# A Fourier, gated-MLP and sigmoid-MLP chain on one core: the mask copies one step earlier, the two readers of a first-layer bank swapped, and a Newton step in three operations

## The chip, the cores and the metric

One core of a Trainium2 chip runs one program. The metric is the device time of one execution in microseconds (us), median of the runs shown. TensorE (PE in the profile) multiplies matrices into PSUM banks, VectorE (DVE), ScalarE (ACT) and GpSimd (POOL) do the elementwise work, and SyncE (SP) issues most of the DMAs. Each engine works through its own list in order, and waits on semaphores for the others.

## The reference, cut to what matters

```python
X = fft(fft(x, axis=1), axis=2).real          # 4 x 3072 x 256
h = relu(X @ w_in)                            # 1024 columns
u, v = h[..., :512], h[..., 512:]
v_n = (v - mean(v)) / sqrt(var(v) + 1e-6)     # over the 512 columns
v_s = einsum('ts,bsd->btd', w_spatial, v_n) + b_spatial[None, :, None]
y = (u * v_s) @ w_out                         # 12288 tokens x 256
out = (sigmoid(y @ w_gate) * (y @ w_val)) @ w_out2
```

## The kernel before

Every fp32 product is made of three matmuls of a high and a low part (`mm3`, L260 to L262). The program has three stages: the Fourier transform with the first layer and its normalization, the spatial product (with `w_out`), and the second MLP. The change touches the first stage alone.

In the first stage the tokens of each of the four batches are handled in four units (3, 2, 0, 1, in this order). A unit has v blocks (128 tokens by 512 columns of v, PSUM tile `psv`) and u blocks (128 columns of u by 384 tokens, `psu`), alternating; one block is one step, 7 or 8 to a unit, 29 to a batch, 116 in all. The transform of real data is symmetric, so a unit holds pairs of tokens k and S - k: the sum of an even part E and an odd part O gives one token, and 2E - (E + O) gives the other. Each block therefore has three parts, that `put_off` spreads over the steps:

- at step n: `mm3` with the even part into the bank and one matmul for the few masked samples (`nt` by `g3`, L588 for a v block, L620 for a u block); ScalarE copies E out (`ev` L595, `eu` L622);
- at step n + 2 (`LAG`), `second`: `mm3` with the odd part adds into the same bank; then ScalarE reads the bank (L602 Relu for v, L628 copy for u), and VectorE reads it for the other token (`mirror`, L580);
- at step n + 3: for a v block `rest`, in which ScalarE puts the mirrored tile through Relu (L608) and VectorE takes the statistics of both tiles (`bn_stats`, L610); for a u block the store.

At the start of a unit ScalarE writes `nt`, a copy of the samples scaled by the batch's mask (L570, one buffer for all units). After a unit, `ln1`, `root` and `ln2` make the mean and the reciprocal root on tiles of 128x6 or 128x7: `y` starts as a reciprocal (L648), one Newton step refines it (L650 to L653), and `nm` is minus mean times `y` (L654). Then the tiles are normalized, the first and the last on ScalarE (L663), the others on VectorE (L659), and stored.

Between the blocks of one batch, the inputs of the next are folded on GpSimd (`fold_half`), split into parts (`split_one`: ScalarE casts `fh`, L255; for the third of a batch four copies `ex` come first, L345 to L348; GpSimd subtracts for `fl`, L256), and transformed (`fft`, `take_fft`). The numbers FOLDS, SPLITS, AT0 and the like give the steps at which these happen; nothing reorders them later. Two readers of one PSUM bank on different engines are put in order by semaphores: who comes first in the program reads first.

The spatial product starts on TensorE when the last block's second part is done (`bank` tiles); its first operands are prepared by `prepare_next` from step 103 on.

Of the kernel before, what the change touches and what calls it, by code (L numbers as in the profile page):

```python
# [10 lines left out]
F32R = mybir.dt.float32r  # L11
# [3 lines left out]
AF = mybir.ActivationFunctionType  # L15
ALU = mybir.AluOpType
# [8 lines left out]
P = 128  # L25
H = 384
R3 = H + 2
# [211 lines left out]
def tile_kernel(ctx: ExitStack, tc: tile.TileContext, t: dict, out: bass.AP):  # L239
    nc = tc.nc  # L240
# [9 lines left out]
    def f(ap):  # L250
        return ap.bitcast(F32)
# [66 lines left out]
    masks = keep.tile([P, 3 + B], F32, name="masks")  # L318
    gc = [keep.tile([P, 2, DFF], F32R, name=f"g{n}") for n in "hl"]
    g3 = keep.tile([P, DFF], F32R, name="g3")  # L320
    nts = [keep.tile([P, R3 if unit == 3 else H], F32R, name=f"nt{unit}") for unit in range(4)]
# [168 lines left out]
    for q, e in ((0, es), (1, xs[:, :, 1, :])):  # L490
        nc.scalar.copy(sps[:, :, q, :], e)
        nc.vector.scalar_tensor_tensor(
            out=sps[:, :, q, :], in0=f(sps[:, :, q, :]), scalar=masks[:, 2:3], in1=e, op0=ALU.mult, op1=ALU.add
# [63 lines left out]
    stp = pool(r0, "stp", 2, "right")  # L557
    vp = pool(r0, "vp", 13, "right")
    up = pool(r0, "up", 3, "right")

    def unit_blocks(pq, b, unit):

        (ph, pl), (qh, ql) = pq

        queue = nc.gpsimd if b == B - 1 and unit < 2 else nc.sync
        vsl = slice(DH, DFF)

        nt = stp.tile([P, R3], F32R, tag="nt", name="nt", bufs=1)
        nt = nt[:, : R3 if unit == 3 else H]
        nc.scalar.activation(nt, f(nts[unit]), AF.Identity, scale=masks[:, 3 + b : 4 + b])  # L570
        nb = 7 if unit == 3 else 6
        tiles = {}
        stats = stp.tile([P, 7, 6], F32, name="stats")
        mv = stp.tile([P, 7, 2], F32, name="mv")
        ve, sd, y, nm = (stp.tile([P, 7], F32, name=n) for n in ("ve", "sd", "y", "nm"))

        def mirror(to, part, ps):
            nc.vector.scalar_tensor_tensor(out=to, in0=part, scalar=2.0, in1=ps, op0=ALU.mult, op1=ALU.subtract)  # L580

        def v_block(m):

            w0 = m * P if m < 3 else R3 - P
            win = slice(w0, w0 + P)
            ps = ps_w.tile([P, 512], F32, tag="pa", name="psv")
            mm3(ps, (ph[:, win], pl[:, win]), (gc[0][:, 0, vsl], gc[1][:, 0, vsl]), True, False)
            nc.tensor.matmul(out=ps, lhsT=nt[:, win], rhs=g3[:, vsl], start=False, stop=True)  # L588
            if m == 3:
                tv = vp.tile([P, DH], F32, tag="tv", name="tv")  # L590
                nc.scalar.activation(tv, ps, AF.Relu)
                tiles[6] = tv
                return lambda: lambda: nc.vector.bn_stats(stats[:, 6, :], tv)
            ev = stp.tile([P, DH], F32, tag="e", name="ev", bufs=4)
            nc.scalar.copy(ev, ps)  # L595

            def second():
                weights = (gc[0][:, 1, vsl], gc[1][:, 1, vsl])
                mm3(ps, (qh[:, win], ql[:, win]), weights, False, True, skip_group_check=True)
                for sg in range(2):  # L600
                    tiles[sg * 3 + m] = vp.tile([P, DH], F32, tag="tv", name="tv")
                nc.scalar.activation(tiles[m], ps, AF.Relu)  # L602
                mirror(tiles[3 + m], ev, ps)
                return rest

            def rest():
                tv = tiles[3 + m]
                nc.scalar.activation(tv, tv, AF.Relu)  # L608
                for sg in range(2):
                    nc.vector.bn_stats(stats[:, sg * 3 + m, :], tiles[sg * 3 + m])  # L610

            return second

        def u_block(fb):

            fsl = slice(fb * P, fb * P + P)
            n = R3 if unit == 3 else H
            ps = ps_w.tile([P, 512], F32, tag="pa", name="psu")
            mm3(ps[:, :n], (gc[0][:, 0, fsl], gc[1][:, 0, fsl]), (ph[:, :n], pl[:, :n]), True, False)
            nc.tensor.matmul(out=ps[:, :n], lhsT=g3[:, fsl], rhs=nt[:, :n], start=False, stop=True)  # L620
            eu = stp.tile([P, R3], F32, tag="e", name="eu", bufs=4)
            nc.scalar.copy(eu[:, :n], ps[:, :n])  # L622

            def second():
                weights = (gc[0][:, 1, fsl], gc[1][:, 1, fsl])
                mm3(ps[:, :H], weights, (qh[:, :H], ql[:, :H]), False, True, skip_group_check=True)
                tu = up.tile([P, 2, H], F32, tag="tu", name="tu")
                nc.scalar.copy(tu[:, 0, :], ps[:, :H])  # L628
                mirror(tu[:, 1, :], eu[:, :H], ps[:, :H])
                if unit == 3:  # L630
                    nc.vector.tensor_copy(tu[:, 1, 0:1], eu[:, H : H + 1])
                at = u_d[b][:, fb, unit * 2 * H : unit * 2 * H + 2 * H]
                return lambda: queue.dma_start(at, tu.rearrange("p a k -> p (a k)"))

            return second

        a = slice(0, nb)

        def ln1():
            for i in range(nb):  # L640
                nc.vector.bn_aggr(mv[:, i, :], stats[:, i, :])
            nc.vector.tensor_scalar(out=ve[:, a], in0=mv[:, a, 1], scalar1=1e-6, scalar2=None, op0=ALU.add)

        def root():
            nc.scalar.activation(sd[:, a], ve[:, a], AF.Sqrt)

        def ln2():
            nc.vector.reciprocal(y[:, a], sd[:, a])  # L648

            nc.vector.tensor_tensor(out=sd[:, a], in0=y[:, a], in1=y[:, a], op=ALU.mult)  # L650
            nc.vector.tensor_tensor(out=sd[:, a], in0=sd[:, a], in1=ve[:, a], op=ALU.mult)
            nc.vector.tensor_scalar(out=sd[:, a], in0=sd[:, a], scalar1=-0.5, scalar2=1.5, op0=ALU.mult, op1=ALU.add)
            nc.vector.tensor_tensor(out=y[:, a], in0=y[:, a], in1=sd[:, a], op=ALU.mult)  # L653
            nc.vector.scalar_tensor_tensor(out=nm[:, a], in0=mv[:, a, 0], scalar=-1.0, in1=y[:, a], op0=ALU.mult, op1=ALU.mult)  # L654

        def norm(i):
            tv = tiles[i]
            if NORM_ON[i] != "a":
                engines[NORM_ON[i]].tensor_scalar(  # L659
                    out=tv, in0=tv, scalar1=y[:, i : i + 1], scalar2=nm[:, i : i + 1], op0=ALU.mult, op1=ALU.add  # L660
                )
            else:
                nc.scalar.activation(tv, tv, AF.Identity, scale=y[:, i : i + 1], bias=nm[:, i : i + 1])  # L663

        def store(i):
            tv = tiles[i]
            if i == 6:
                q = H - (R3 - P)
                queue.dma_start(v_d[b][0:1, unit * 6 + 3, :], tv[q : q + 1, :])
            elif unit == 3 and i == 3:  # L670

                for rows in (slice(16, P), slice(1, 16)):
                    queue.dma_start(v_d[b][rows, unit * 6 + i, :], tv[rows, :])
            else:
                queue.dma_start(v_d[b][:, unit * 6 + i, :], tv)

        def norms(i):
            for k in (i, i + 3):
                norm(k)
            for k in (i, i + 3):  # L680
                store(k)

        def last_norm():
            norm(6)
            store(6)

        blocks = []
        for i in range(4):
            if i < nb - 3:
                blocks.append(lambda i=i: v_block(i))  # L690
            blocks.append(lambda i=i: u_block(i))
        after = [root, ln2] + [lambda i=i: norms(i) for i in range(3)] + ([last_norm] if nb == 7 else [])
        return blocks, [ln1] + after
# [94 lines left out]
    units = [(b, unit) for b in range(B) for unit in (3, 2, 0, 1)]  # L788
# [41 lines left out]
    seconds, thirds, lns = {}, {}, {}  # L830
    step = 0

    def put_off(step, block=None):

        if block is not None:
            seconds[step + LAG] = block()
        if step in seconds:
            thirds[step + 1] = seconds.pop(step)()
        if step in thirds:
            thirds.pop(step)()  # L840
# [41 lines left out]
            for q in range(2):  # L882
                transform(base + AT3[q], b + 1, 3, q, pqs[b + 1, 3], None)
    transform(NYQ, B, 0, 0, None, None)
    for b, unit in units:
        blocks, later = unit_blocks(pqs[b, unit], b, unit)
        for block in blocks:
            put_off(step, block)
            for do in plan.pop(step, []):
                do()  # L890
            for first, _ in ffts.get(step, []):
                first()
            for do in lns.pop(step, []):
                do()
            for _, take in ffts.get(step, []):
                take()
            step += 1
        for k, do in enumerate(later):
            lns.setdefault(step + LAG + k, []).append(do)
# [457 lines left out]
```

## Time and profile before

| | us |
|---|---|
| median of 3 runs (2971.44 to 2974.28) | 2972.27 |
| the profiled execution | 2973.02 |
| its span | 2971.2 |
| PE busy | 2867.2 (96%) |
| DVE busy | 2064.7 (69%) |
| ACT busy | 1323.5 (45%) |
| POOL busy | 401.2 (14%) |

These are times of the whole span. The stages differ: TensorE is without pauses in the second and third, and VectorE is the busiest engine in the first. A share of the span thus says little on the change, and the rows below are taken from stretches of the first stage. "busy" is the time in which an engine executes, the idle time ahead of an instruction is put down to what ended it, and instructions of one engine overlap a little, so that the start of the next comes before the end of the last.

### The profile page before, as it was taken

The numbers are of one execution on the slowest core, as the hardware profiler recorded it, in microseconds if no ns is written. First come the engines' busy times: TensorE is split into PE (matmuls) and PEld (weight loads), VectorE is DVE, ScalarE is ACT, GpSimd is POOL, SyncE is SP. The second block draws the span as 40 slices with busy tenths as digits, with TensorE's granted clock in tenths as the row PEclk, the third lists the DMA queues.
The fourth block names the chain that finished last, engine by engine and source line by source line (L and its number), as shares of the span: only waits on it lengthen the run. The fifth ranks groups of instructions, "written<-read, shape, count | busy, mean of one in ns | idle before, by whom it ended". The sixth has DMA issues, their size and how long they took to land.

```text
span 2971.2 us, 34046 instructions
## 1 busy us (share of the span) xinstructions
PE 2867.2 (96%) x12550; PEld 2359.4 (79%) x12550; DVE 2064.7 (69%) x2908; ACT 1323.5 (45%) x2117; POOL 401.2 (14%) x408
## 2 busy tenths in 40 slices
PE   3888899999999999999999999999999999999999
PEld 2777788888878888888887888788888888888887
DVE  8898875768765765576666476866666666766665
ACT  3777532323232232332223233655555555555554
POOL 5774121122111002111002010000000000000000
PEclk8999999999999999999999999999999999999999
DMA  6565875778765776776876474200000000000000
GB/s 230 187 235 221 313 276 196 278 244 316 264 221 175 260 252 211 242 257 222 282 259 223 154 271 166 84 29 29 29 10 20 29 29 29 15 15 29 29 15 15
DMA packets 149656, 472.28 MB, mean 159 GB/s; under 512 B 16624, under 2 KB 18160, under 8 KB 149104
## 3 DMA queue, kind: packets, MB, share of 16 engines
q1 hardware_dynamic: 143712, 442.70, 43.2%
q0 software_dynamic: 2320, 14.82, 1.3%
q10 hardware_dynamic: 3456, 12.58, 1.1%
q8 instruction: 98, 1.61, 0.2%
q14 instruction: 70, 0.57, 0.1%
HBM read 387.46 MB, written 82.58 MB: 158 GB/s over the span
## 4 chain that ended last, share of the span: by engine, by line
PE 87%; DVE 8%; ACT 2%; issue 2%; DMA 1%; ACTq 0%; DVEq 0%; SPq 0%
PE bank L261 28%; PE bank L262 28%; PE bank L260 28%; DVE stats L610 1%; DVE gl L994 1%; DVE g L986 1%; ACT wh L751 1%; DVE st L747 1%; DVE tv L580 0%; DVE wl L754 0%; DVE tu L580 0%; DMA v_d<-tv 0%; PE psv L588 0%; DVE tv L659 0%; PE psf L260 0%
## 5 line engine op out<-in xcount | busy, mean ns | idle before, releaser
L262 PE MATMUL bank<-wh,vl 128*128 128x512 f32 x2016 | 786.3, 390 | 0.0
L261 PE MATMUL bank<-wl,vh 128*128 128x512 f32 x2016 | 786.0, 390 | 0.0
L260 PE MATMUL bank<-wh,vh 128*128 128x512 f32 x2016 | 785.4, 390 | 0.0
L754 DVE TENSOR_TENSOR wl<-st,wh 128x1024 fp32r<-128x1024 f32 x252 | 331.4, 1315 | 390.9 <-ACT wh L751 388.9
L751 ACT CAST wh<-st 128x1024 fp32r<-128x1024 f32 x252 | 265.2, 1053 | 594.6 <-PE bank L262 351.6
L260 PEld LDWEIGHTS bank<-wh,vh 128*128 128x128 f32 x2016 | 379.3, 188 | 79.9
L261 PEld LDWEIGHTS bank<-wl,vh 128*128 128x128 f32 x2016 | 379.1, 188 | 80.0
L262 PEld LDWEIGHTS bank<-wh,vl 128*128 128x128 f32 x2016 | 378.9, 188 | 79.0
L1240 DVE TENSOR_TENSOR t<-t,bank 128x512 f32<-128x512 f32 x144 | 99.0, 688 | 250.3 <-PE bank L262 250.2
L747 POOL TENSOR_TENSOR st<-st 128x1024 f32<-128x1024 f32 x60 | 156.5, 2608 | 812.9 <-DMA st<-v_d 512.2
L261 PE MATMUL bank<-x,wgh 128*128 128x512 f32 x673 | 265.9, 395 | 0.0
L262 PE MATMUL bank<-x,wgl 128*128 128x512 f32 x673 | 265.5, 395 | 0.0
L260 PE MATMUL bank<-x,wgh 128*128 128x512 f32 x673 | 264.1, 392 | 0.4 <-ACT t L1252 0.4
L747 DVE TENSOR_TENSOR st<-st 128x1024 f32<-128x1024 f32 x180 | 226.1, 1256 | 53.9 <-DMA st<-in_wt 53.9
L1261 DVE TENSOR_TENSOR gl<-s,gh 128x512 fp32r<-128x512 f32 x288 | 199.4, 693 | 57.4 <-ACT gh L1259 44.5
L262 PE MATMUL bank<-gh,wv 128*128 128x512 f32 x576 | 227.6, 395 | 0.0
L260 PE MATMUL bank<-gh,wv 128*128 128x512 f32 x576 | 226.8, 394 | 0.8 <-ACT gh L1254 0.8
L261 PE MATMUL bank<-gl,wv 128*128 128x512 f32 x576 | 225.8, 392 | 0.2 <-DVE gl L1261 0.2
L1231 ACT ACTIVATE s<-s 128x512 f32<-128x512 f32 x144 | 91.0, 632 | 149.0 <-DVE s L1230 149.0
L260 PEld LDWEIGHTS bank<-x,wgh 128*128 128x128 f32 x673 | 126.4, 188 | 31.2 <-ACT t L1252 0.8
L261 PEld LDWEIGHTS bank<-x,wgh 128*128 128x128 f32 x673 | 126.3, 188 | 30.6
L262 PEld LDWEIGHTS bank<-x,wgl 128*128 128x128 f32 x673 | 126.2, 188 | 28.6
(233 smaller groups left out, 4564.2 us busy)
## 6 DMA issues: line engine op xcount, KB each, us to landing
st<-in_wt SPq DMA_DIRECT2D x432, 512.0 KB, 5.3
st<-v_d SPq DMA_DIRECT2D x144, 512.0 KB, 4.9
u<-u_d SPq DMA_DIRECT2D x96, 256.0 KB, 4.4
u_d<-tu SPq DMA_DIRECT2D x56, 384.0 KB, 3.1
v_d<-tv SPq DMA_DIRECT2D x80, 256.0 KB, 2.5
xt<-in_xh SPq DMA_DIRECT2D x24, 512.0 KB, 4.6
x_d<-x ACTq DMA_DIRECT2D x24, 512.0 KB, 3.2
raw<-x_d SPq DMA_DIRECT2D x24, 512.0 KB, 4.5
```

The source lines that it names most:

```text
L260: nc.tensor.matmul(out=ps, lhsT=w[0], rhs=x[0], start=first, stop=False, **kw)
L261: nc.tensor.matmul(out=ps, lhsT=w[0], rhs=x[1], start=False, stop=False, **kw)
L262: nc.tensor.matmul(out=ps, lhsT=w[1], rhs=x[0], start=False, stop=last, **kw)
L610: nc.vector.bn_stats(stats[:, sg * 3 + m, :], tiles[sg * 3 + m])
L747: (nc.gpsimd if kind == "v" else nc.vector).tensor_tensor(out=tiles[0], in0=tiles[0], in1=tiles[1], op=ALU.add if sign > 0 else ALU.subtract)
L751: nc.scalar.copy(hl[0], tiles[0])
L754: lows.append(lambda: nc.vector.tensor_tensor(out=hl[1], in0=tiles[0], in1=f(hl[0]), op=ALU.subtract))
L986: nc.vector.scalar_tensor_tensor(out=g, in0=side["u"][d], scalar=0.0, in1=g, op0=ALU.max, op1=ALU.mult)
L994: side["low"] = lambda: nc.vector.tensor_tensor(out=gl, in0=g, in1=f(gh), op=ALU.subtract)
L1231: nc.scalar.activation(s1, s1, AF.Sigmoid)
L1240: nc.vector.tensor_tensor(out=g["t2"], in0=g["t2"], in1=g["b"], op=ALU.add)
L1261: nc.vector.tensor_tensor(out=l, in0=s, in1=f(h), op=ALU.subtract)
```

## The change

`own_samples` takes the writing of `nt` out of `unit_blocks`; it is called right behind the first part of the last block of the unit before (for the first unit ahead of the loop). In `second` of both kinds of block `mirror` stands ahead of ScalarE's read of the bank. The four operations of the Newton step become three, with the factor and the 1.5 folded into `scalar_tensor_tensor`.

```diff
@@ -558,16 +558,21 @@
     vp = pool(r0, "vp", 13, "right")
     up = pool(r0, "up", 3, "right")
 
+    nt_of = {}
+
+    def own_samples(b, unit):
+
+        nt = stp.tile([P, R3], F32R, tag="nt", name="nt", bufs=1)[:, : R3 if unit == 3 else H]
+        nc.scalar.activation(nt, f(nts[unit]), AF.Identity, scale=masks[:, 3 + b : 4 + b])
+        nt_of[b, unit] = nt
+
     def unit_blocks(pq, b, unit):
 
         (ph, pl), (qh, ql) = pq
 
         queue = nc.gpsimd if b == B - 1 and unit < 2 else nc.sync
         vsl = slice(DH, DFF)
-
-        nt = stp.tile([P, R3], F32R, tag="nt", name="nt", bufs=1)
-        nt = nt[:, : R3 if unit == 3 else H]
-        nc.scalar.activation(nt, f(nts[unit]), AF.Identity, scale=masks[:, 3 + b : 4 + b])
+        nt = nt_of.pop((b, unit))
         nb = 7 if unit == 3 else 6
         tiles = {}
         stats = stp.tile([P, 7, 6], F32, name="stats")
@@ -599,8 +604,8 @@
                 mm3(ps, (qh[:, win], ql[:, win]), weights, False, True, skip_group_check=True)
                 for sg in range(2):
                     tiles[sg * 3 + m] = vp.tile([P, DH], F32, tag="tv", name="tv")
+                mirror(tiles[3 + m], ev, ps)
                 nc.scalar.activation(tiles[m], ps, AF.Relu)
-                mirror(tiles[3 + m], ev, ps)
                 return rest
 
             def rest():
@@ -625,8 +630,8 @@
                 weights = (gc[0][:, 1, fsl], gc[1][:, 1, fsl])
                 mm3(ps[:, :H], weights, (qh[:, :H], ql[:, :H]), False, True, skip_group_check=True)
                 tu = up.tile([P, 2, H], F32, tag="tu", name="tu")
+                mirror(tu[:, 1, :], eu[:, :H], ps[:, :H])
                 nc.scalar.copy(tu[:, 0, :], ps[:, :H])
-                mirror(tu[:, 1, :], eu[:, :H], ps[:, :H])
                 if unit == 3:
                     nc.vector.tensor_copy(tu[:, 1, 0:1], eu[:, H : H + 1])
                 at = u_d[b][:, fb, unit * 2 * H : unit * 2 * H + 2 * H]
@@ -645,13 +650,13 @@
             nc.scalar.activation(sd[:, a], ve[:, a], AF.Sqrt)
 
         def ln2():
+            stt = nc.vector.scalar_tensor_tensor
             nc.vector.reciprocal(y[:, a], sd[:, a])
 
-            nc.vector.tensor_tensor(out=sd[:, a], in0=y[:, a], in1=y[:, a], op=ALU.mult)
-            nc.vector.tensor_tensor(out=sd[:, a], in0=sd[:, a], in1=ve[:, a], op=ALU.mult)
-            nc.vector.tensor_scalar(out=sd[:, a], in0=sd[:, a], scalar1=-0.5, scalar2=1.5, op0=ALU.mult, op1=ALU.add)
-            nc.vector.tensor_tensor(out=y[:, a], in0=y[:, a], in1=sd[:, a], op=ALU.mult)
-            nc.vector.scalar_tensor_tensor(out=nm[:, a], in0=mv[:, a, 0], scalar=-1.0, in1=y[:, a], op0=ALU.mult, op1=ALU.mult)
+            stt(out=ve[:, a], in0=y[:, a], scalar=-0.5, in1=ve[:, a], op0=ALU.mult, op1=ALU.mult)
+            nc.vector.tensor_tensor(out=ve[:, a], in0=ve[:, a], in1=y[:, a], op=ALU.mult)
+            stt(out=y[:, a], in0=ve[:, a], scalar=1.5, in1=y[:, a], op0=ALU.add, op1=ALU.mult)
+            stt(out=nm[:, a], in0=mv[:, a, 0], scalar=-1.0, in1=y[:, a], op0=ALU.mult, op1=ALU.mult)
 
         def norm(i):
             tv = tiles[i]
@@ -830,10 +835,12 @@
     seconds, thirds, lns = {}, {}, {}
     step = 0
 
-    def put_off(step, block=None):
+    def put_off(step, block=None, also=None):
 
         if block is not None:
             seconds[step + LAG] = block()
+            if also is not None:
+                own_samples(*also)
         if step in seconds:
             thirds[step + 1] = seconds.pop(step)()
         if step in thirds:
@@ -882,10 +889,11 @@
             for q in range(2):
                 transform(base + AT3[q], b + 1, 3, q, pqs[b + 1, 3], None)
     transform(NYQ, B, 0, 0, None, None)
-    for b, unit in units:
+    own_samples(*units[0])
+    for (b, unit), follows in zip(units, units[1:] + [None]):
         blocks, later = unit_blocks(pqs[b, unit], b, unit)
         for block in blocks:
-            put_off(step, block)
+            put_off(step, block, follows if block is blocks[-1] else None)
             for do in plan.pop(step, []):
                 do()
             for first, _ in ffts.get(step, []):
```

ScalarE at the end of batch 0's unit 0, the 7th and 8th row of each list being where `nt` for unit 1 (`nt1`) is written; `eu`, `tu` and `tv` are the copies of E, of u and of v. Before:

```order
L622 COPY eu_1058<-psu_1053 128x384 [waits DVE_49,PE_49]
L628 COPY tu_1063<-psu_1011 128x384 [waits DMAHW2_49,PE_49]
L608 ACTIVATE tv_1039<-tv_1039 128x512 [waits DMAHW7_49,DVE_49]
L663 ACTIVATE tv_759<-tv_759,nm_710,y_709 128x512 [waits DVE_49]
L622 COPY eu_1078<-psu_1073 128x384 [waits PE_49,Activation_49]
L602 ACTIVATE tv_1083<-psv_1028 128x512 [waits DMAHW0_49,PE_49]
L570 ACTIVATE nt_1092<-nt1_135,masks_130 128x384
L595 COPY ev_1105<-psv_1100 128x512 [waits DVE_49,PE_49]
L628 COPY tu_1110<-psu_1053 128x384 [waits DMAHW4_49,PE_49]
```

The same place of ScalarE's list now (numbers of buffers differ by a few):

```order
L627 COPY eu_1056<-psu_1051 128x384 [waits PE_49,Activation_49]
L634 COPY tu_1061<-psu_1010 128x384 [waits DMAHW2_49,DVE_49]
L613 ACTIVATE tv_1038<-tv_1038 128x512 [waits DMAHW6_49]
L668 ACTIVATE tv_759<-tv_759,nm_710,y_709 128x512 [waits DVE_49]
L627 COPY eu_1076<-psu_1071 128x384 [waits PE_49,Activation_49]
L566 ACTIVATE nt_1078<-nt1_135,masks_130 128x384
L608 ACTIVATE tv_1083<-psv_1027 128x512 [waits DMAHW1_49,DVE_49]
L600 COPY ev_1103<-psv_1098 128x512 [waits PE_49]
L634 COPY tu_1108<-psu_1051 128x384 [waits DMAHW4_49,DVE_49]
```

`nt` has moved up by one instruction, the Relu of a v tile; the normalization that waits for VectorE (L663, now L668) still stands ahead of it. The reads of `psu` and `psv` for `tu` and `tv` waited for PE and now wait for DVE.

VectorE at the same place; `stats` are the statistics of the two v tiles of one block, the second of which ScalarE has put through Relu (`tv_1039` before, `tv_1038` now) behind its copy of `tu`. Before:

```order
L580 SCALAR_TENSOR_TENSOR tu_1063<-eu_1016,psu_1011 128x384 [waits DMAHW2_49,Activation_49]
L610 BN_STATS stats_943<-tv_1038 128x6
L610 BN_STATS stats_943<-tv_1039 128x6 [waits Activation_49]
L659 TENSOR_SCALAR tv_760<-tv_760,y_709,nm_710 128x512 [waits DVE_49]
L580 SCALAR_TENSOR_TENSOR tv_1084<-ev_1033,psv_1028 128x512 [waits DMAHW1_49,Activation_49]
```

Now:

```order
L585 SCALAR_TENSOR_TENSOR tu_1061<-eu_1015,psu_1010 128x384 [waits DMAHW2_49,PE_49]
L615 BN_STATS stats_942<-tv_1037 128x6 [waits Activation_49]
L615 BN_STATS stats_942<-tv_1038 128x6 [waits Activation_49]
L664 TENSOR_SCALAR tv_760<-tv_760,y_709,nm_710 128x512 [waits DVE_49]
L585 SCALAR_TENSOR_TENSOR tv_1084<-ev_1032,psv_1027 128x512 [waits DMAHW0_49,PE_49]
```

VectorE's own order is the same. The mirrors waited for ScalarE and now wait for TensorE; the statistics, which follow at once, wait for ScalarE as before, and ScalarE's instructions ahead of that now wait for the mirror.

## Rows read from the trace of the kernel before

**Rows 1.** The page's span.

```profile
span 2971.2 us, 34046 instructions
```

**Rows 2.** Windows: stretch, its length, busy us by engine, PE clock, DMA share, GB/s.

```profile
200.00:300.00 100.00, 88.06 (x428) 78.94 (x427) 90.06 (x215) 72.18 (x146) 50.63 (x75) 0.95 0.61 221
...
1000.00:1500.00 500.00, 499.48 (x2198) 412.12 (x2197) 326.07 (x356) 146.77 (x168) 55.38 (x26) 1.00 0.72 243
```

**Rows 3.** Timeline of PE where the stages meet: start, duration, instruction [idle before <-releaser].

```profile
343.86 0.44 PE L260 MATMUL psu<-ph,gh 128*128 128x384 f32 x1 [1.71 <-ACT eu L622]
...
344.49 0.39 PE L260 MATMUL bank<-wh,vh 128*128 128x512 f32 x1
```

**Rows 4.** Timeline of ACT just before that.

```profile
342.63 0.81 ACT L663 ACTIVATE tv<-tv,nm,y 128x512 f32<-128x512 f32 x1 [0.79 <-DVE nm L654]
343.35 0.46 ACT L622 COPY eu<-psu 128x384 f32<-128x384 f32 x1
```

**Rows 5.** Timeline of DVE just before that.

```profile
342.43 0.17 DVE L654 SCALAR_TENSOR_TENSOR nm<-mv,y 128x6 f32<-128x6 f32 x1
```

**Rows 6.** Waits of DVE, 0 to 420 us: total us, times, longest us.

```profile
DVE tv L580 <- ACT tv L602: 19.0, 11, 3.4
DVE tu L580 <- ACT tu L628: 9.2, 13, 1.5
```

**Rows 7.** Waits of PE, 0 to 420 us.

```profile
PE psv L588 <- ACT nt L570: 34.3, 16, 6.3
```

**Rows 8.** Timeline of ACT at the end of batch 1's unit 0.

```profile
187.80 0.81 ACT L663 ACTIVATE tv<-tv,nm,y 128x512 f32<-128x512 f32 x1 [2.33 <-DVE nm L654]
...
188.88 0.60 ACT L602 ACTIVATE tv<-psv 128x512 f32<-128x512 f32 x1
189.37 0.61 ACT L570 ACTIVATE nt<-nt,masks 128x384 fp32r<-128x384 f32 x1
```

**Rows 9.** Timeline of PE at that place.

```profile
190.03 0.80 PE L588 MATMUL psv<-g,nt 128*128 128x512 f32 x1 [4.60 <-ACT nt L570]
```

**Rows 10.** Timeline of DVE, a mirror of u, two statistics, a mirror of v.

```profile
199.81 0.54 DVE L580 SCALAR_TENSOR_TENSOR tu<-eu,psu 128x384 f32<-128x384 f32 x1
200.28 1.27 DVE L610 BATCH_NORM_STATS2 stats<-tv 128x6 f32<-128x512 f32 x2
201.48 0.66 DVE L580 SCALAR_TENSOR_TENSOR tv<-ev,psv 128x512 f32<-128x512 f32 x1
```

**Rows 11.** Timeline of ACT, the copy of u and the Relu behind it.

```profile
207.48 0.48 ACT L628 COPY tu<-psu 128x384 f32<-128x384 f32 x1
207.86 0.64 ACT L608 ACTIVATE tv<-tv 128x512 f32<-128x512 f32 x1
```

**Rows 12.** Timeline of ACT, a cast that DVE waits for.

```profile
300.81 0.48 ACT L421 CAST ph<-psf 128x384 fp32r<-128x384 f32 x1 [1.65 <-DVE even L862]
```

**Rows 13.** Timeline of DVE, the instruction released by that cast.

```profile
301.32 0.56 DVE L422 TENSOR_TENSOR pl<-psf,ph 128x384 fp32r<-128x384 f32 x1 [0.55 <-ACT ph L421]
```

**Rows 14.** Lines, 60 to 345 us: count, ns min/median/max, first and last start.

```profile
L610 DVE BATCH_NORM_STATS2 stats<-tv x94: 668/679/691, 80.2 to 343.6; 128x6 f32<-128x512 f32 x94
L654 DVE SCALAR_TENSOR_TENSOR nm<-mv,y x15: 165/167/1147, 102.3 to 342.4; 128x6 f32<-128x6 f32 x11, 128x7 f32<-128x7 f32 x4
```

**Rows 15.** Timeline of DVE, two operations of a Newton step.

```profile
272.17 0.17 DVE L650 TENSOR_TENSOR sd<-y 128x6 f32<-128x6 f32 x1
272.37 0.17 DVE L651 TENSOR_TENSOR sd<-sd,ve 128x6 f32<-128x6 f32 x1
```

**Rows 16.** Timeline of DVE, the same operation beside GpSimd's work.

```profile
184.88 2.28 DVE L651 TENSOR_TENSOR sd<-sd,ve 128x6 f32<-128x6 f32 x1
```

**Rows 17.** Timeline of POOL at that place.

```profile
182.41 4.72 POOL L256 TENSOR_TENSOR fl<-fo,fh 128x1024 fp32r<-128x1024 f32 x2
```

**Rows 18.** Timeline of ACT, the cast behind the four copies of a split.

```profile
196.33 1.05 ACT L255 CAST fh<-fo 128x1024 fp32r<-128x1024 f32 x1
```

**Rows 19.** Timeline of DVE behind it.

```profile
198.39 0.69 DVE L580 SCALAR_TENSOR_TENSOR tv<-ev,psv 128x512 f32<-128x512 f32 x1 [2.94 <-ACT tv L602]
```

## The prediction

> **What bounds the kernel now.** I read the windows first. In the spatial product TensorE is busy for 499 of 500 us; in the first stage it is busy for 88 of 100 and VectorE for 90, with ScalarE at 72 [rows 2]. From the first `bank` matmul, at 344.49, TensorE has next to nothing to wait for [rows 2, 3]. So the change can only move that moment: what the first stage wins or loses is won or lost by the whole, and the 96% of TensorE's share tell nothing of it.
>
> Then I went back from that moment. The last second part waits for the copy of `eu` [rows 3], which ScalarE makes behind its normalization, which waits for `nm` of VectorE [rows 4, 5]. `nm` starts at 342.43 because VectorE comes to it then in its list. VectorE's progress therefore dates the end of the stage. Between 70 and 343 us it is nearly always at work, apart from 24 waits of 28.2 us in all ahead of a mirror, each for ScalarE's read of the same bank [rows 6].
>
> TensorE's waits for `nt` look larger, 34.3 us in 16 places [rows 7], but they are waits of an engine that runs ahead of the one that decides. They count only where VectorE then finds its bank unfinished.
>
> **Part 1: `nt` earlier.** The order shows `nt` moved up past one Relu of 0.60 and, where a transform is taken in the same step, past two casts as well. At the end of unit 0, where the largest stalls are, nothing else lies between: ScalarE stands at the normalization until 187.80, waiting 2.33 us for `nm`, and that is still ahead of `eu` and `nt` [rows 8]. So `nt` would start some 0.5 us earlier, at 188.88 for 189.37, and the 4.60 us stall [rows 9] keeps about 4.1. The added `nt` itself is no new work (16 before, 16 after); it now stands ahead of the Relu, which reaches the mirrored tile later by its 0.6. Value: 0.5 us at the about 8 of 16 boundaries where VectorE soon runs out of finished banks, 4 us gained. Bounds: 0, if VectorE is never short of banks, and 34.3.
>
> **Part 2: the mirror first.** What it removes: at each of the 24 waits the mirror no longer stands behind ScalarE's read. It still waits for TensorE, so where TensorE or ScalarE's backlog is late, only the read itself drops out: 0.48 for a copy [rows 11], 0.60 for a Relu [rows 8], with 0.03 for the hand-over (a cast starts at 300.81 and lasts 0.48, the next on VectorE starts at 301.32 [rows 12, 13]). 24 by 0.55 is 13.2 us. The upper bound is all 28.2.
>
> What it adds is not in the list of edits. Before, ScalarE ran ahead: it had copied u and put the mirrored v tile through Relu long before VectorE came to the mirror, and the two statistics ran behind it without a gap [rows 10]; no wait of the statistics is in the list of VectorE's waits. Now ScalarE's copy of u waits for the mirror of u, the Relu stands behind that copy, and the second statistic waits for the Relu. Put times to it from the mirror's start: mirror done at 0.54, copy started at 0.57, Relu 0.38 later at 0.95 [rows 11], done at 1.59, second statistic at 1.62. Without the wait it starts 0.47 (the mirror's) and 0.60 (half of 1.20 for the pair) after, at 1.07 [rows 10]. So each pair costs 0.55 us more on the engine that decides. There are 94 statistics in 47 pairs, 46 of them ahead of the last `nm` [rows 14]: 25.3 us. Behind VectorE's waiting statistic stand the next mirror and the normalizations; behind ScalarE's waiting copy stand the next `ev` or `eu`, which TensorE needs two steps later, so TensorE is not held. Some pairs lie where VectorE would have waited anyway; I take one in ten off: 23. Bounds: 0, if the idle places hide all, and 25.3.
>
> A rule bears on this. The hand-over from ScalarE to VectorE is seen at each of the 24 waits [rows 6]. The Trainium skill (PSUM — Partial Sum Buffer, section on bank collisions) says that two engines must not read one bank at the same time, that the hardware doesn't hold one back, and that software has to guard it. The trace agrees as far as it goes. Without such a guard both reads would start together, the new wait would be nothing, and the sum would be a gain of about 20; the order, in which ScalarE's read now waits for DVE, rules that out.
>
> Nor do all the long waits go. The wait of 2.94 at 198.39 [rows 19] stands behind ScalarE's four copies and its cast, which ends at 197.38 [rows 18]. The mirror can now start without them, at 195.45. But the next statistics need the Relu of the v tile, which stays behind that cast: 197.38, then some 0.5 for `ev` and 0.60 for the Relu, so the pair begins near 198.5, where before it began at 200.28 [rows 10]; its own 0.55 and a later start of the four copies (they now follow a copy of u that waits for a mirror) leave about 1 of the 2.94. This is why I take 13.2 and not 28.2.
>
> **Part 3: Newton.** Four operations become three. Their pace is 0.20 [rows 15], and a `scalar_tensor_tensor` of this shape has a median of 0.167 [rows 14], no more than the operations it replaces. 15 units come ahead of the last `nm`: 3.0 us gained. An operation of this step can also be held by GpSimd: 2.28 instead of 0.17, and it ended at 187.16, when GpSimd's two subtractions ended, at 187.13 [rows 15 to 17]. `nm`, a `scalar_tensor_tensor`, shows 1.147 at the most [rows 14], so the new form is not free of it. Bounds: 0, if VectorE merely reaches the next held operation sooner, and 3.0 and one such excess of 2.1.
>
> The Trainium skill (SBUF — State Buffer, Who interferes with whom) calls this an exclusive lock between GpSimd and a VectorE operation with two SBUF inputs. The three new operations still have two each; by that rule the excess stays and 3.0 is all, without it the excess of 2.1 would come on top.
>
> **The sum.** -4 (`nt`), -13.2 (old waits), -3.0 (Newton), +23 (new waits): 2.8 us slower. The profiled execution took 2973.02 (span 2971.2 [rows 1], the rest lies around it), 0.75 above the median of 2972.27. From it: 2975.8; on the median's scale 2975.
>
> **Rivals.**
>
> *The old waits really go.* If the 28.2 us vanish whole, with Newton's 3.0, and 15 of the new 25.3 remain, the change gains 16: 2956. For it: VectorE's waits are where it loses most, and its idle stretches can hide new waits. It also gives GpSimd free time in the new waits, and so fewer held operations. Against: the new waits, if they come at every pair, are nearly as long as all the old ones together, and they fall where VectorE is not idle now.
>
> *ScalarE in step with VectorE.* Slower: in the copies and casts of a split ScalarE cannot work ahead any more, since its copy of u waits for a mirror; the first statistic of the next pair waits about 2 us each of the three times, on top of all 46 new waits. 25.3 + 6 - 13.2 - 3.0 is 15 slower: 2987. It decides from the point where the pairs' waits pass the sum of what goes, 20 us, or 37 of 46 pairs at 0.55. For it: VectorE has 90 of 100 us of work. Against: the waits that go overlap with some of them.
>
> *`nt` doesn't come earlier.* TensorE's stalls at the end of unit 0 stay, because the normalization is still ahead, and `nt` gains nothing: -13.2 - 3.0 + 23, 6.8 slower: 2979. For it rows 8; against it that the other 12 boundaries have casts or more Relus ahead.
>
> **How the numbers follow.** The forecast has 50% (its own range 2966 to 2983), the first rival 20%, the second 20%, the third 10%. A measurement tells this kernel from no change by 0.2%, 5.9 us: 2966.3 to 2978.2 is the same. Of the forecast's half 40 points lie in there, 8 above, 2 below; the first rival gives 18 to faster and 2 to the same; the second all but 2 to slower; the third 4 to the same and 6 to slower. Faster 20%, same 48%, slower 32%. The range takes the forecast and the third whole and about half of the first and of the second: 2959 to 2987.
>
> **What would show it.** Waits of VectorE's statistics for ScalarE's Relu, near 46 of about 0.55, absent before. The waits ahead of mirrors nearly gone from the list. TensorE's waits for `nt` still there at the end of unit 0, above 3 us each, and below 1 us elsewhere. The first `bank` matmul near 347. Newton's operations three to a unit at a pace of 0.20. I am wrong if the statistics do not wait, if the stalls at the ends of unit 0 vanish with `nt`, or if the spatial product begins more than 6 us from 344.5; wrong in the premise if it begins where I say and the end moves otherwise.

## The result and the profile after

The changed kernel takes 2991.48 us (median of 4 runs, 2988.07 to 2993.9), the kernel before 2973.28 in the same comparison: a ratio of 1.0061, 95% interval 1.0043 to 1.0078, 18.2 us slower. The forecast was 2975, in a range up to 2987.

The loss is in the first stage. Its end, the first `bank` matmul, stood at 344.49 [rows 3]. After:

```profile
365.04 0.63 PE L260 MATMUL bank<-wh,vh 128*128 128x512 f32 x1
```

It comes 20.6 us later, and the span is 20.9 longer. VectorE's account of the stretch from 64 us to that moment, as windows (length, then busy us of PE, PEld, DVE, ACT, POOL), of the kernel before:

```profile
64.00:344.49 280.49, 236.22 (x1123) 210.89 (x1124) 236.53 (x547) 197.49 (x395) 150.05 (x227) 0.94 0.61 219
```

And after:

```profile
64.00:365.04 301.04, 245.33 (x1123) 215.52 (x1124) 233.01 (x536) 193.28 (x396) 150.34 (x229) 0.92 0.57 204
```

VectorE works 3.5 us less in all (236.53 to 233.01) and stands still 24.1 us more (43.96 to 68.03). TensorE has the same 1123 matmuls but is busy 9 us more, at a mean granted clock of 0.92 for 0.94: it waits 30 times, where it waited 23 times, and runs at the lower of its two levels behind some of them (1.2 GHz, a granted clock of 0.50, from 365.04 to 367, where the `bank` matmul takes 0.63 for 0.39). That alone is not the loss: newton_only, below, has 0.92 as well, and its first `bank` matmul comes at 344.39.

What VectorE waited for in that stretch after the change (total us, times, longest):

```profile
DVE stats L615 <- ACT tv L613: 25.1, 47, 1.5
DVE stats L615 <- ACT tv L608: 8.3, 6, 2.6
DVE pl L422 <- ACT ph L421: 8.0, 7, 3.4
DVE tv L585 <- PE psv L262: 6.3, 6, 2.9
...
DVE tu L585 <- PE psu L262: 2.4, 6, 0.7
DVE even L869 <- PE psf L262: 1.9, 2, 1.0
```

The 28.2 us of waits for ScalarE's reads of the banks [rows 6] are gone to the last one. The first line is the new wait of the pairs: 47 times 0.53, where 46 times 0.55 was worked out. The other lines are new or have grown (the casts `ph` cost 3.7 us before, `even` 0.5); the sum did not have them, or had them as a rival alone. ScalarE shows why:

```profile
ACT tu L634 <- DVE tu L585: 63.1, 51, 3.4
ACT tv L608 <- DVE tv L585: 24.5, 34, 1.2
```

ScalarE stands 87.6 us at banks that VectorE has yet to read. In the kernel before none of its reads of a bank waited for VectorE: it had a lead there, and VectorE used it. It did wait for VectorE at other instructions, first of all at normalizations and casts; all its waits for VectorE in the stretch add up to 39.7 us before and to 95.1 now. One pair, VectorE first, then ScalarE:

```profile
201.82 0.55 DVE L585 SCALAR_TENSOR_TENSOR tu<-eu,psu 128x384 f32<-128x384 f32 x1 [0.50 <-PE psu L262]
202.29 0.69 DVE L615 BATCH_NORM_STATS2 stats<-tv 128x6 f32<-128x512 f32 x1
203.44 0.69 DVE L615 BATCH_NORM_STATS2 stats<-tv 128x6 f32<-128x512 f32 x1 [0.47 <-ACT tv L613]
```

```profile
202.40 0.48 ACT L634 COPY tu<-psu 128x384 f32<-128x384 f32 x1 [0.89 <-DVE tu L585]
202.78 0.63 ACT L613 ACTIVATE tv<-tv 128x512 f32<-128x512 f32 x1
```

The mirror ends at 202.37, the copy starts at 202.40, the Relu ends at 203.41, the second statistic starts at 203.44: the loop as forecast, 0.47 idle (0.55 counted from the start that the pair had before). A little later comes a split, ScalarE first:

```profile
205.54 0.48 ACT L634 COPY tu<-psu 128x384 f32<-128x384 f32 x1 [1.75 <-DVE tu L585]
206.04 0.41 ACT L345 COPY ex<-fo 64x256 f32<-64x256 f32 x1
...
207.80 1.04 ACT L255 CAST fh<-fo 128x1024 fp32r<-128x1024 f32 x1
...
209.23 0.60 ACT L608 ACTIVATE tv<-psv 128x512 f32<-128x512 f32 x1
```

```profile
204.96 0.55 DVE L585 SCALAR_TENSOR_TENSOR tu<-eu,psu 128x384 f32<-128x384 f32 x1
...
206.75 0.55 DVE L585 SCALAR_TENSOR_TENSOR tu<-eu,psu 128x384 f32<-128x384 f32 x1
209.86 0.69 DVE L615 BATCH_NORM_STATS2 stats<-tv 128x6 f32<-128x512 f32 x1 [2.56 <-ACT tv L608]
```

ScalarE can begin its 2.8 us of copies and cast only when VectorE has mirrored u (at 204.96); VectorE does its next mirror, at 206.75, and then has nothing until the Relu behind them. The wait of 2.94 [rows 19] has come back as one of 2.56 at another instruction.

TensorE's waits for the mask copy fell from 34.3 us [rows 7] to 27.0. The largest, 6.3 before, is still there, at the end of batch 3's unit 0:

```profile
349.10 0.80 PE L593 MATMUL psv<-g,nt 128*128 128x512 f32 x1 [5.22 <-ACT nt L566]
```

### The profile page after: what moved, and what is told of

It reads as the page before. It is cut to its first block, busy times and chain, and to the rows that moved or that the text cites. A ratio compares the mean times of both kernels' runs of the same rounds, so it can differ in the third digit from the quotient of the medians.

```text
span 2992.1 us, 33981 instructions
## 1 busy us (share of the span) xinstructions
PE 2876.2 (96%) x12550; PEld 2364.2 (79%) x12550; DVE 2069.0 (69%) x2892; ACT 1318.7 (44%) x2117; POOL 399.9 (13%) x408
## 4 chain that ended last, share of the span: by engine, by line
PE 88%; DVE 7%; ACT 3%; issue 2%; DMA 0%; ACTq 0%; DVEq 0%
PE bank L261 28%; PE bank L262 28%; PE bank L260 28%; DVE tv L664 1%; ACT tv L613 1%; DVE st L752 1%; DVE tu L585 1%; DVE gl L1002 1%; DVE g L994 0%; PE psf L260 0%; PE psu L260 0%; DVE tv L585 0%; PE psf L262 0%; DVE wl L759 0%; PE psf L261 0%
```

## The experiments

Times are medians; each is compared with runs of the kernel before (2972.1 to 2972.4, for the change itself 2973.3). The diffs are cut, with "..." for what is left out; the line above each says what the kernel is.

| kernel | us | ratio to before, 95% interval |
|---|---|---|
| the change | 2991.48 | 1.0061 [1.0043, 1.0078] |
| swap_only | 3013.27 | 1.0136 [1.0120, 1.0151] |
| no_swap | 2961.47 | 0.9960 [0.9946, 0.9975] |
| swap_v_only | 2972.14 | 0.9997 [0.9988, 1.0007] |
| swap_u_only | 3026.32 | 1.0182 [1.0168, 1.0196] |
| rest_first | 2993.41 | 1.0069 [1.0054, 1.0084] |
| nt_only | 2964.29 | 0.9977 [0.9966, 0.9988] |
| newton_only | 2970.84 | 0.9995 [0.9986, 1.0004] |
| late_read | 2971.43 | 0.9996 [0.9987, 1.0006] |
| late_read_but_end | 2972.32 | 1.0005 [0.9996, 1.0014] |
| norm_later | 2965.09 | 0.9976 [0.9966, 0.9985] |

**swap_only**: `nt` and the Newton step as before, the swap kept.

```diff
-            put_off(step, block, follows if block is blocks[-1] else None)
+            put_off(step, block)
...
+        own_samples(b, unit)
         nt = nt_of.pop((b, unit))
...
```

> The mirror ahead of ScalarE's read in both kinds of block, with the mask copies and the Newton step as they were before. Theory: all of the loss is the swap's, since the second statistic of each pair now waits for two ScalarE instructions that stand behind the mirror; so this is slower than before by 20 to 26 us (the 18 measured for the change and the 3 to 6 that the two other edits give back), with statistics waiting near 34 us in all. Rival: the loss comes from the mask copy, which now stands ahead of a Relu that VectorE needs, or from the new Newton operations; then this is within 6 us of before.

41 us slower, far more than the 20 to 26 expected, but on the theory's side. The statistics wait as in the change (25.1 and 8.4 us). TensorE's waits for `nt`, 34.3 us before [rows 7], have grown, and so have VectorE's waits for TensorE ahead of the mirrors of u, 2.4 us in the change:

```profile
PE psv L594 <- ACT nt L566: 55.6, 16, 8.2
```

```profile
DVE tu L586 <- PE psu L262: 18.0, 16, 2.1
```

At its old place `nt` has at least one more of ScalarE's reads ahead of it, and these now stand still at the banks, so it comes later yet. The two other edits thus give back some 22 us beside the swap, and half as much without it (no_swap): the parts of the change do not add up.

**no_swap**: the change with ScalarE's read first again.

```diff
-                mirror(tiles[3 + m], ev, ps)
                 nc.scalar.activation(tiles[m], ps, AF.Relu)
+                mirror(tiles[3 + m], ev, ps)
...
-                mirror(tu[:, 1, :], eu[:, :H], ps[:, :H])
                 nc.scalar.copy(tu[:, 0, :], ps[:, :H])
+                mirror(tu[:, 1, :], eu[:, :H], ps[:, :H])
```

> The mask copies a step ahead and the Newton step in three operations, with ScalarE's read first as before. Theory: 3 to 8 us faster than before: 3.0 to 3.5 from 16 operations fewer, 0 to 4 from TensorE's shorter waits; statistics don't wait. Rival (the loss is of these two): 12 us or more slower than before.

10.8 us faster than before, more than the 3 to 8 expected, and 30 faster than the change: the swap is the loss, and its price is larger than the whole. No statistic waits. It is the fastest kernel of this study.

```profile
DVE tv L585 <- ACT tv L607: 20.6, 13, 3.4
...
DVE tu L585 <- ACT tu L633: 4.3, 9, 1.2
```

The first `bank` matmul comes 6.8 us earlier than before:

```profile
337.65 0.39 PE L260 MATMUL bank<-wh,vh 128*128 128x512 f32 x1
```

The other 4.6 us by which the span is shorter lie behind it, where none of the edits reaches. TensorE is busy 3.3 us less there, with the same 11377 matmuls; why is not shown.

**swap_v_only**: the change with ScalarE's read first in the u blocks alone.

```diff
-                mirror(tu[:, 1, :], eu[:, :H], ps[:, :H])
                 nc.scalar.copy(tu[:, 0, :], ps[:, :H])
+                mirror(tu[:, 1, :], eu[:, :H], ps[:, :H])
```

> All of the change but the u blocks, in which ScalarE reads first as before. Theory: the wait of the second statistic comes from the copy of u that waits for the mirror of u, so the 25.6 us of these waits go, while the 19.0 us of waits ahead of the mirrors of v stay gone; the three or so waits of 2.6 us for the Relu behind the splits' casts stay. 2960 to 2975. Rival: any wait of ScalarE for VectorE takes its lead away, and with the v blocks alone most of the loss stays: 2982 to 2990.

2972, within the theory's range, and 10.7 above no_swap. No statistic waits here, not even behind the splits' casts, where the theory had three such waits stay. The waits ahead of the mirrors of v for ScalarE are gone, 20.6 us in no_swap, and those of u have grown from 4.3, because ScalarE's copy of u stands behind a Relu that waits for VectorE:

```profile
DVE tu L585 <- ACT tu L633: 27.6, 33, 2.1
```

```profile
ACT tv L608 <- DVE tv L585: 55.3, 43, 3.2
```

So the waits of the pairs hang on the u blocks, and yet the swap costs without them: the waits taken off at v came back at u.

**rest_first**: the whole change, the Relu and the statistics of a step ahead of the next mirror.

```diff
+        if step in thirds:
+            thirds.pop(step)()
         if step in seconds:
             thirds[step + 1] = seconds.pop(step)()
-        if step in thirds:
-            thirds.pop(step)()
```

> The whole change, and in each step the Relu of the mirrored tile and the two statistics (rest) stand ahead of the second part, so ahead of the next mirror and of ScalarE's copy of u; nothing else differs. Theory: the pairs' waits of 25.6 us go, because the Relu no longer stands behind a copy that waits for a mirror; 2962 to 2975. Rival: ScalarE being in step with VectorE costs as much in the splits, where its four copies and the cast stand, and for the transforms' casts; then the pairs' waits go, but the time stays above 2982.

2993.4: nothing won. This is the run that contradicts the theory in its first form, by which the 25 us of the pairs were the loss. They fall to 14.4, not to nothing, and the time comes back at the first statistic, the transforms' casts and the mirrors. ScalarE's waits at the banks do not fall: 93.3 us, 9.9 of them at v, for 89.0 in the change over the same 420 us:

```profile
DVE stats L615 <- ACT tv L613: 14.4, 22, 1.2
DVE tv L585 <- PE psv L262: 13.1, 11, 2.9
DVE pl L422 <- ACT ph L421: 12.2, 14, 3.4
DVE stats L615 <- ACT tv L608: 12.1, 11, 2.4
```

```profile
ACT tu L634 <- DVE tu L585: 83.4, 62, 4.5
```

The time is the rival's, above 2982, though it had the pairs' waits go, and they only fell by less than half. By the rival, what costs is that ScalarE has to stand at the banks, wherever VectorE then meets it; the next run tests that.

**late_read**: a new theory from that. The whole change, with ScalarE's read one step behind the mirror, and the Relu, the statistics and the stores one step later still.

```diff
                 mirror(tiles[3 + m], ev, ps)
-                nc.scalar.activation(tiles[m], ps, AF.Relu)
-                return rest
+                return read
+
+            def read():
+                nc.scalar.activation(tiles[m], ps, AF.Relu)
+                return rest
...
```

> The whole change, but ScalarE's read of the bank comes a step after the mirror (and the Relu, the statistics and the store one more step later), so that ScalarE finds the mirror done. Theory: the loss comes from ScalarE having to stand at each bank until VectorE has read it, which takes its lead away; with a step between them that wait is gone and the time falls to that without the swap, 2956 to 2968, with ScalarE's waits for mirrors below 30 us (89 in the change). Rival: any read of ScalarE behind VectorE's ties the two together, or banks and tiles held a step longer cost as much: above 2980.

20 us faster than the change, and not the 2956 to 2968 expected: 2971.4, level with before. VectorE still reads first, and the waits on both sides are mostly gone (stretch of 64 to 340 us):

```profile
DVE stats L618 <- ACT tv L616: 5.5, 11, 0.9
```

```profile
ACT tu L642 <- DVE tu L585: 15.8, 17, 1.4
```

The first `bank` matmul comes at 334.7, 10 us earlier than before and 3 earlier than in no_swap. Then TensorE meets a bank that the first layer still holds, and the matmul behind the wait takes 0.79, where 0.39 is usual [rows 3]:

```profile
343.38 0.79 PE L260 MATMUL bank<-wh,vh 128*128 128x512 f32 x1 [5.07 <-ACT tu L642]
```

It waits for a copy of u that starts at 342.85, and that one for VectorE, which prepares operands of the spatial product from 335.58 on and then normalizes before it comes to the mirror:

```profile
342.22 0.55 DVE L585 SCALAR_TENSOR_TENSOR tu<-eu,psu 128x384 f32<-128x384 f32 x1
```

So the same order of the two readers can do without most of the loss, if neither has to stand and wait for the other. That it then costs nothing is not shown: the time stays 10 us above no_swap.

**late_read_but_end**: the same, with ScalarE's read at once behind the mirror in the last unit.

```diff
+        at_end = b == B - 1 and unit == 1
...
-                return read
+                return at_once(read) if at_end else read
...
```

> As late_read, but in the last unit of all ScalarE reads at once behind the mirror. In late_read the first bank matmul came at 334.7, 10 us before the kernel before, and TensorE then waited 5.1 us for ScalarE's last copy of u, whose bank it takes over, and ran cold behind it. Theory: that wait at the seam is all that hides the gain of the late read; without it the time is 2957 to 2963, level with no_swap or a little below. Rival: the late read itself costs as much as it saves (tiles and banks held longer); the time stays at 2968 to 2974.

The theory on the seam, the place where the two stages meet, fails: 2972.3. The wait at the bank is 6.36 us in the trace (of an execution of 2980, the slowest of eleven), since here as in late_read VectorE prepares operands of the spatial product between its mirrors and reaches the last mirrors of u late. In no_swap its last mirror of u comes at 347.60, and yet TensorE waits for no bank; why is not shown. How much the late read would win without that seam stays open.

**swap_u_only**: the change with ScalarE's read first in the v blocks alone.

```diff
-                mirror(tiles[3 + m], ev, ps)
                 nc.scalar.activation(tiles[m], ps, AF.Relu)
+                mirror(tiles[3 + m], ev, ps)
```

> All of the change but the v blocks, in which ScalarE reads first as before. No swap took 2961.5, the v blocks' swap alone added 10.7, both add 30. Theory (the pair's wait hangs on the copy of u alone): 18 to 26 us above no_swap, 2980 to 2988, and the statistics wait in nearly all 48 pairs. Rival (the two only cost together, ScalarE losing its lead for good when it has to stand at every bank): 2965 to 2975.

3026, 65 us above no_swap: twice the swap of both, and neither theory had it. Each engine now waits for the other within every two steps:

```profile
DVE tv L585 <- ACT tv L607: 56.1, 47, 4.4
DVE stats L615 <- ACT tv L613: 20.5, 48, 0.5
```

```profile
ACT tu L634 <- DVE tu L585: 117.1, 62, 3.9
```

The same split as above, VectorE and then ScalarE:

```profile
222.31 0.55 DVE L585 SCALAR_TENSOR_TENSOR tu<-eu,psu 128x384 f32<-128x384 f32 x1
227.22 0.69 DVE L585 SCALAR_TENSOR_TENSOR tv<-ev,psv 128x512 f32<-128x512 f32 x1 [4.36 <-ACT tv L607]
```

```profile
222.89 0.48 ACT L634 COPY tu<-psu 128x384 f32<-128x384 f32 x1 [1.76 <-DVE tu L585]
...
225.15 1.05 ACT L255 CAST fh<-fo 128x1024 fp32r<-128x1024 f32 x1
...
226.58 0.60 ACT L607 ACTIVATE tv<-psv 128x512 f32<-128x512 f32 x1
```

ScalarE waits 1.76 for the mirror of u, does its copies, cast and Relu, and VectorE waits 4.36 for that Relu. One engine works at a time. The swap of the v blocks takes away this second wait, so that beside the swap of u it saves 35 us, and alone it costs 10.7.

**newton_only**: the new Newton step alone, so no_swap without the earlier `nt`.

```diff
-            put_off(step, block, follows if block is blocks[-1] else None)
+            put_off(step, block)
...
+        own_samples(b, unit)
         nt = nt_of.pop((b, unit))
...
```

> The Newton step in three operations alone; the mask copies and the two readers as before. It shares with nt_only the 10.8 us that both won together. Theory: 3 to 4 us faster than before, the 3.5 us that VectorE had less to do in the first stage with the change. Rival: fewer operations are also held by GpSimd less often, and TensorE gets its mask copy sooner behind a shorter chain; then 6 to 10 us.

1.3 us faster, which its interval (4.2 faster to 1.2 slower) does not tell from nothing, nor from the 3 to 4 expected; 6 to 10 it excludes. In the trace of the change the three operations take 0.167 in the median, as the four did, and each can still be held:

```profile
L658 DVE SCALAR_TENSOR_TENSOR y<-ve,y x15: 166/167/1148, 100.9 to 360.9; 128x6 f32<-128x6 f32 x11, 128x7 f32<-128x7 f32 x4
```

The median hides most of the time. In the kernel before, one of the four operations has a median of 0.17 and this account over its 16 units (total, then mean ns):

```profile
L651 DVE TENSOR_TENSOR sd<-sd,ve 128x6 f32<-128x6 f32 (+1 forms) x16 | 7.6, 474 | 0.5
```

Up to the first `bank` matmul the four took 21.8 us in the kernel before; the three take 16.8 here, 11.6 in the change and 22.9 in no_swap. What they are held beyond their 0.17, as in [rows 16], is thus more than what one operation fewer saves, and it differs from kernel to kernel.

**nt_only**: the earlier `nt` alone, so no_swap with the Newton step as before.

```diff
-            stt(out=ve[:, a], in0=y[:, a], scalar=-0.5, in1=ve[:, a], op0=ALU.mult, op1=ALU.mult)
-            nc.vector.tensor_tensor(out=ve[:, a], in0=ve[:, a], in1=y[:, a], op=ALU.mult)
-            stt(out=y[:, a], in0=ve[:, a], scalar=1.5, in1=y[:, a], op0=ALU.add, op1=ALU.mult)
+            nc.vector.tensor_tensor(out=sd[:, a], in0=y[:, a], in1=y[:, a], op=ALU.mult)
+            nc.vector.tensor_tensor(out=sd[:, a], in0=sd[:, a], in1=ve[:, a], op=ALU.mult)
+            nc.vector.tensor_scalar(out=sd[:, a], in0=sd[:, a], scalar1=-0.5, scalar2=1.5, op0=ALU.mult, op1=ALU.add)
+            nc.vector.tensor_tensor(out=y[:, a], in0=y[:, a], in1=sd[:, a], op=ALU.mult)
```

> The mask copies a step ahead alone. Theory: 6 to 8 us faster than before, the rest of the 10.8, though at the ends of unit 0 the copy comes only half a microsecond earlier. Rival (those waits of TensorE don't decide, as forecast): within 4 us of before.

7.8 us faster, the theory's size: the place of this copy decides more than was forecast. Of TensorE's 16 waits for it [rows 7] eight are gone, and the total falls by 5.5 us. At the ends of unit 0, where the copy moved least, three of the four have even grown, from 4.2, 4.6 and 5.2 us to 6.9 each. VectorE's waits ahead of the mirrors of u fall from 9.2 to 3.9 us.

```profile
PE psv L593 <- ACT nt L566: 28.8, 8, 6.9
```

**norm_later**: no_swap, with the normalizations and their stores a step later.

```diff
-            lns.setdefault(step + LAG + k, []).append(do)
+            lns.setdefault(step + LAG + k + (k > 2), []).append(do)
```

> No swap, the mask copies and Newton as changed, and the normalizations and their stores one step later, so that ScalarE's normalization stands behind the mask copy instead of ahead of it. Theory: TensorE's waits for the mask copy at the ends of unit 0 come from ScalarE standing at that normalization; they fall from 28.5 to below 10 us in all, and since VectorE decides, the time falls by 0 to 4 us only: 2957 to 2962. Rival: these waits decide: 2950 or less. Or the tiles held longer make the stores late: 2963 or more.

TensorE's waits for `nt` fall to 12.8 us, not quite to the 10 expected, so ScalarE's stand at the normalization is indeed what holds the copy at those places; the first `bank` matmul comes at 332.1. The time is nevertheless 2965.1, 3.6 above no_swap, as the third expectation had it: ScalarE waits for v tiles that are not stored yet, and TensorE waits at the seam for VectorE's last mirror of u.

```profile
PE psv L593 <- ACT nt L566: 12.8, 8, 3.7
...
PE bank L260 <- DVE tu L585: 6.4, 1, 6.4
```

```profile
ACT tv L607 <- DMA v_d<-tv: 11.9, 5, 4.3
```

## Why the prediction was wrong

**Where the loss had to be** held: the first stage alone, dated by the first `bank` matmul, 20.6 of the 20.9 us of the span. It is no date where TensorE stops again behind it, as in late_read and norm_later.

**The new wait** (part 2, +23) held in mechanism, and in size as a sum of waits: 25.1 us in 47 pairs, where 25.3 was worked out and 23 taken. How much of it decided is less clear: in the chain of work that ended last, as the profile infers it, the Relu of these pairs stands 28 times.

**The old waits** (part 2, -13.2) is the step that failed: the swap as a whole, 9.8 us in the sum (-13.2 and +23), costs 30.0 between no_swap and the change, and 41.0 alone. All 28.2 us left the list, more than was taken, but nothing was won by it. In their place stand 8.3 us at the first statistics, 8.7 of mirrors for TensorE and 4.3 more for the transforms' casts; with the other small waits, VectorE's idle time rises by 24.1 us, where the sum of -4, -13.2 and +23 gives 5.8. swap_v_only shows the same without the pairs: 20.6 us of waits at v gone, 23.3 more at u. I priced each wait by the instruction it ended in, and on the one engine that I held to decide. The measured thing is that ScalarE waits 87.6 us at the banks for VectorE, where it had a lead before. In the chain that ended last, from 64 us to the first `bank` matmul, ScalarE's instructions add up to 34.6 us before, 63.5 in the change and 19.1 in no_swap. rest_first shows that taking 11 of the largest line's 25 us away does not bring the time back, and late_read shows that a step between the two readers brings back 20 us with the same order of readers.

With nothing for the old waits the sum would have been 16 slower, near the measured 18.2. That would have been luck in part: the two other edits, 7 us in the sum, give 10.8 without the swap and some 22 beside it.

**The second rival**, ScalarE in step with VectorE, is what came: 2987 against 2991.5. It had the place (the splits) and 2 us for each wait of a first statistic there, measured as 2.56 at one; it was given 20%. Its number is near partly by luck, since it too counted the 13.2 as won. Its argument, that VectorE has 90 of 100 us of work, holds for the window it was read from; over the whole stretch it is 84% (236.53 of 280.49). Here each wait taken off came back at another instruction that needs the engine now bound to VectorE.

**`nt`** (part 1, -4): -7.8 alone. That TensorE's waits there are those of an engine that runs ahead did not hold: of the 16 copies 13 stand in the chain of the kernel before, one of them with the matmul that it releases:

```profile
189.47 0.51 ACT nt L570
190.03 0.80 PE psv L588
```

That the copy at the ends of unit 0 would stay behind the normalization held (2.63 us in the first batch, 3.5 to 5.22 in the others). That elsewhere less than 1 us would stay did not, with 3.76 at 163.20, 4.48 at 240.24 and 1.85 at 310.25, at the ends of unit 3.

```profile
163.20 0.80 PE L593 MATMUL psv<-g,nt 128*128 128x512 f32 x1 [3.76 <-ACT nt L566]
...
240.24 0.50 PE L593 MATMUL psv<-g,nt 128*128 128x512 f32 x1 [4.48 <-ACT nt L566]
```

**Newton** (part 3, -3.0): alone it measured -1.3, not told from zero, with the first `bank` matmul 0.1 earlier. The 3.5 us that VectorE works less in the change are no proof of it. They are a balance. Newton's operations take 10.2 us less, and three operations for four explain 2.5 of it; the rest is that they are held for less time in this trace. The statistics, which no longer follow each other without a gap, take 4.9 more, and the normalizations 2.4 more. The price of 0.20 an operation left out the time for which operations are held.

**The rule on one bank and two readers** (the Trainium skill, PSUM — Partial Sum Buffer, bank collisions) was read rightly: the trace shows the two reads in order in both kernels, 0.03 us apart. A gain of about 20, which the sum would have had without that order, did not come.

## What to carry to other kernels

When two engines must read the same bank in turn, try first to let the one with slack go first (here ScalarE, 70% busy in the stretch, for VectorE's 84%): in this kernel it then worked ahead, and the fuller engine found its inputs ready. If the order must be the other way, put other work between the reads; a step brought back 20 of 30 us here. Before pricing a swap wait by wait, write down for both engines what stands behind the new wait, and whether any of it feeds the other engine: if it does, the waits can come back under other names, and the total waiting of the engine that was made second is the better measure. From 64 us to the first `bank` matmul ScalarE waits for VectorE for 49, 70, 95, 98 and 132 us in no_swap, swap_v_only, the change, rest_first and swap_u_only, and that is also the order of their times.

## What was not expected of the hardware

Nothing of the chip itself, but the size of the coupling: of four versions that differ only in which engine reads first in which kind of block, the times are 2961, 2972, 2991 and 3026 us, and the largest is not the one with both swapped.
